# A fused attention and feed-forward kernel: crossbar transposes from the second batch on, and a new order of the first batch

## The chip, the cores and the metric

The kernel runs on one core of a Trainium2 chip. The metric is the time of one execution on the device, in microseconds (us). Lower is better. Most executions of one kernel agree within a few tenths of a per cent. A comparison always has runs of both kernels on the same chip in the same rounds.

The engines have short names in the profile: PE is the tensor engine, DVE the vector engine, ACT the scalar engine, POOL the engine that issues the loads here, SP the engine that issues stores and crossbar transposes. "Line" numbers such as L468 are lines of the kernel file in question, so they differ between kernels.

## The reference

```
# q, k, v: (8 batches, 12 heads, 448 rows, 64)
scores = q @ k^T / 8
attn   = max(scores, 0)**2 / 448
x      = (attn @ v), heads side by side        # 3584 rows x 768
out    = (max(x @ w_gate, 0) * (x @ w_val)) @ w_out      # 768 -> 1536 -> 768
```

Inputs and output are float32; the kernel computes in bfloat16 with float32 accumulation.

## The kernel before

The kernel has no fixed schedule. It makes a list of operations with their dependences, buffers and estimated durations; a small planner inside the kernel places them in time on paper, and the kernel then emits them in the planned order. Each engine executes its own instructions in exactly that order (in `e1b_head_only` below, DVE stands 4.33 us at one copy with its other work queued behind it), so a wrong estimate in the plan becomes a wait on the chip. This is the planner's part; `xfer` is what it believes that a transfer takes:

```python
def commit(self, op, s, e):
    op.start, op.eng = s, e
    d = op.engs[e]
    self.t[e] = s + d
    op.end = s + d
    if op.xfer:
        if e == "POOL":
            self.dmaq = max(self.dmaq, op.end + 1.3) + op.xfer
            op.end = self.dmaq + 0.7
            # (cut)
        else:
            op.end += 2.0 + op.xfer
```

q and k have to be transposed before the scores. For batches 0 to 2 PE does it (`transpose_quad`, four heads at a time, with a copy out of PSUM on DVE or ACT for each pair of heads). From batch `XBAR_FROM = 3` on the DMA crossbar does it: seven DVE copies bring a batch into pair order in one buffer (`pair`, there is only one), and two crossbar transposes, issued by SP, read it:

```python
def transpose_batch(b):
    # (cut)
    for s, t in enumerate(slot_order(b)):
        op = Op({"DVE": 0.36}, lambda s=s, t=t: emit_pair(s, t), deps=deps + perm[:1], delay=6.0,
                alloc=[pair] if s == 0 else [], reads=[st.buf])      # st.buf: the loaded q and k
        perm.append(op)
        others.append(op)
    # (cut)
    for i in range(2):
        op = Op({"SP": 0.3}, lambda i=i: emit_x(i), deps=perm + xo[:1], alloc=[st.tbuf] if i == 0 else [],
                reads=[pair], xfer=13.0)                              # the plan believes 2 + 13 us
        xo.append(op)
        others.append(op)
    for hp in range(HP):
        t_op[(b, hp)] = xo[1]                                         # scores wait for the second
```

There are two input buffers for q and k (`r_in = Res(2)`). The load of batch b+2 may start when batch b has been transposed, or, with the crossbar, when its seven copies are done.

After attention come the FFN products: groups of six matrix products (`g_ps`, `v_ps`) and groups of twelve (`o_ps`). They are PE's reserve of work for the times when attention has to wait; the FFN of a batch needs all value products of that batch.

## Time and profile before

| | before |
|---|---|
| time, median of 3 | 443.87 us (443.56 to 444.12) |
| span of the profiled execution | 442.0 us |
| PE busy | 428.8 us (97%) |
| batch 1's first transposes start | 37.99 us |
| PE's waits after that | one, 0.51 us |

The page's table of engines, and the row of the 40 slices for PE (each digit is the busy share of a slice of 11 us in tenths):

```profile
PE 428.8 (97%) x3092; PEld 228.9 (52%) x3092; DVE 222.2 (50%) x392; ACT 210.2 (48%) x354; POOL 44.2 (10%) x65
...
PE   6799999999999999999999999999999999999996
```

PE is the limit everywhere but in the first slices and the last. A change gains by giving PE less to do, or by a shorter head. PE's timeline (start, length, instructions; in brackets the idle time before and what ended it) shows the head, two groups of transposes, and the only later wait:

```profile
5.17 0.96 PE L332 MATMUL t_ps<-ident,qk 128*64 128x128 bf16 x14 [0.31 <-issue]
7.25 0.96 PE L332 MATMUL t_ps<-ident,qk 128*64 128x128 bf16 x14 [1.12 <-DMA qk<-in_q_dram]
...
9.20 0.98 PE L456 MATMUL s_ps<-qkT 64*128 64x192 bf16 x10 [0.72 <-ACT qkT L340]
11.98 1.70 PE L332 MATMUL t_ps<-ident,qk 128*64 128x128 bf16 x28 [1.80 <-DMA qk<-in_q_dram]
...
37.99 0.95 PE L332 MATMUL t_ps<-ident,qk 128*64 128x128 bf16 x28
...
62.17 0.95 PE L332 MATMUL t_ps<-ident,qk 128*64 128x128 bf16 x28
63.05 0.67 PE L554 MATMUL g_ps<-xT,wg_99 128*128 128x192 bf16 x6
```

```profile
142.95 0.37 PE L456 MATMUL s_ps<-qkT 64*128 64x448 bf16 x2 [0.51 <-ACT xT L525]
```

A length includes the time in which one group's end overlaps the next, so the cost of a group is read from start to start: the 28 transposes at 62.17 us cost 63.05 - 62.17 = 0.88 us. The same 28 at 11.98 us cost nearly twice as much, 1.64 us to the next start: PE ran at half rate there. (The view of stretches gives the granted clock as 1.00 from 12 to 14 us; the durations of the same instructions are the surer sign here.)

SP's timeline around the first crossbar transposes (batch 3's; the length is the time SP needs to hand them to the DMA engines, not the time to landing):

```profile
102.97 18.29 SPq L376 DMA_TRANSPOSE qkT<-pair  x2
...
183.18 4.33 SPq L376 DMA_TRANSPOSE qkT<-pair  x1
```

The view of the tile that these transposes read gives their landing: issued at 103.0 us amid loads, 15.6 us later; the second, at 107.8 us, 25.3 us later; the one at 183.2 us, with few loads around it, 6.6 us later.

### The profile page before, as it was taken

The numbers are of one execution on the slowest core, as the hardware profiler recorded it, in microseconds if no ns is written. First come the engines' busy times: TensorE is split into PE (matmuls) and PEld (weight loads), VectorE is DVE, ScalarE is ACT, GpSimd is POOL, SyncE is SP. The second block draws the span as 40 slices with busy tenths as digits, with TensorE's granted clock in tenths as the row PEclk, the third lists the DMA queues.
The fourth block names the chain that finished last, engine by engine and source line by source line (L and its number), as shares of the span: only waits on it lengthen the run. The fifth ranks groups of instructions, "written<-read, shape, count | busy, mean of one in ns | idle before, by whom it ended". The sixth has DMA issues, their size and how long they took to land.

```text
span 442.0 us, 7571 instructions
## 1 busy us (share of the span) xinstructions
PE 428.8 (97%) x3092; PEld 228.9 (52%) x3092; DVE 222.2 (50%) x392; ACT 210.2 (48%) x354; POOL 44.2 (10%) x65
## 2 busy tenths in 40 slices
PE   6799999999999999999999999999999999999996
PEld 2577775545454444544455444554445544555553
DVE  1676865656707654645753646635553456302210
ACT  3675656654536544544554555444553444332221
POOL 8336220004001100020001000010000000000000
PEclk9999999999999999999999999999999999999999
DMA  7999999707996990499044901390002200040014
GB/s 101 191 198 198 202 203 203 160 14 73 175 170 176 166 156 0 83 194 154 1 63 116 161 1 29 75 182 21 1 1 73 71 1 0 1 104 5 1 37 107
DMA packets 69699, 42.76 MB, mean 97 GB/s; under 512 B 29088, under 2 KB 66208, under 8 KB 69664
## 3 DMA queue, kind: packets, MB, share of 16 engines
q0 software_dynamic: 37824, 24.38, 39.2%
q1 hardware_dynamic: 31760, 17.80, 21.5%
q8 instruction: 24, 0.39, 0.4%
q10 hardware_dynamic: 80, 0.10, 0.1%
q14 instruction: 11, 0.09, 0.1%
HBM read 48.76 MB, written 11.01 MB: 135 GB/s over the span
## 4 chain that ended last, share of the span: by engine, by line
PE 95%; DMA 2%; DVE 1%; POOL 1%; ACT 1%; issue 0%; POOLq 0%; DVEq 0%
PE g_ps L554 26%; PE o_ps L606 25%; PE v_ps L554 25%; PE s_ps L513 7%; PE s_ps L456 7%; PE t_ps L332 2%; PE s_ps L462 2%; DMA qk<-in_q_dram 2%; PE s_ps L507 1%; POOL qk L239 1%; ACT xT L525 0%; DVE at L490 0%; DVE qkT L342 0%; DVE r_sb L474 0%; DVE o_sb L621 0%
## 5 line engine op out<-in xcount | busy, mean ns | idle before, releaser
L472 ACT ACTIVATE r_sb<-s_ps 128x896 bf16<-128x896 f32 (+5 forms) x161 | 107.3, 726 | 34.0 <-PE s_ps L456 19.7
L568 DVE TENSOR_TENSOR hT<-v_ps,g_sb 128x448 bf16<-128x448 f32 (+2 forms) x108 | 61.6, 570 | 113.4 <-PE v_ps L554 109.3
L490 DVE TENSOR_TENSOR at<-r_sb 128x896 bf16<-128x896 bf16 (+4 forms) x171 | 98.2, 609 | 24.2 <-ACT r_sb L472 24.0
L561 ACT ACTIVATE g_sb<-g_ps 128x448 bf16<-128x448 f32 (+2 forms) x104 | 53.1, 510 | 99.2 <-PE g_ps L554 97.0
L606 PEld LDWEIGHTS <-hT 128*128 128x128 bf16 x672 | 63.9, 98 | 48.5 <-issue 7.7
L474 DVE TENSOR_SCALAR r_sb<-s_ps 128x896 bf16<-128x896 f32 (+4 forms) x58 | 52.8, 933 | 38.0 <-PE s_ps L456 38.0
L619 ACT ACTIVATE o_sb<-o_ps 128x384 f32<-128x384 f32 (+1 forms) x55 | 26.8, 488 | 69.9 <-PE o_ps L606 68.9
L606 PE MATMUL o_ps<-wo_106,hT 128*128 128x384 bf16 x336 | 59.3, 326 | 0.0
L606 PE MATMUL o_ps<-wo_107,hT 128*128 128x384 bf16 x336 | 59.2, 326 | 0.0
L456 PE MATMUL s_ps<-qkT 64*128 64x448 bf16 (+2 forms) x324 | 38.1, 343 | 1.8 <-ACT qkT L340 0.7
L513 PE MATMUL s_ps<-at,vv 128*64 128x448 bf16 (+2 forms) x324 | 33.4, 345 | 0.0
L239 POOL DMA_DIRECT2D vv<-in_v_dram x20 | 14.2, 719 | 185.3 <-PE s_ps L513 140.7
L525 ACT CAST xT<-s_ps 128x896 bf16<-128x896 f32 (+2 forms) x26 | 21.7, 835 | 17.0 <-PE s_ps L513 17.0
L456 PEld LDWEIGHTS <-qkT 64*128 64x128 bf16 x324 | 12.4, 97 | 22.0 <-issue 15.9
L513 PEld LDWEIGHTS <-vv 128*64 128x64 bf16 x324 | 16.3, 113 | 14.5 <-issue 7.5
L554 PE MATMUL g_ps<-xT,wg_94 128*128 128x448 bf16 (+2 forms) x108 | 21.2, 333 | 0.0
L554 PE MATMUL g_ps<-xT,wg_96 128*128 128x448 bf16 (+2 forms) x108 | 21.2, 332 | 0.0
L554 PE MATMUL g_ps<-xT,wg_99 128*128 128x448 bf16 (+2 forms) x108 | 21.2, 332 | 0.0
L554 PE MATMUL g_ps<-xT,wg_97 128*128 128x448 bf16 (+2 forms) x108 | 21.2, 332 | 0.0
L554 PE MATMUL g_ps<-xT,wg_95 128*128 128x448 bf16 (+2 forms) x108 | 21.2, 332 | 0.0
L554 PE MATMUL g_ps<-xT,wg_98 128*128 128x448 bf16 (+2 forms) x108 | 21.2, 332 | 0.0
L554 PE MATMUL v_ps<-xT,wv_101 128*128 128x448 bf16 (+2 forms) x108 | 21.2, 332 | 0.0
(55 smaller groups left out, 336.8 us busy)
## 6 DMA issues: line engine op xcount, KB each, us to landing
out_dram<-o_sb SPq DMA_DIRECT2D x54, 192.0 KB, 2.7
vv<-in_v_dram POOLq DMA_DIRECT2D x14, 384.0 KB, 10.1
qk<-in_k_dram POOLq DMA_DIRECT2D x6, 672.0 KB, 15.8
qk<-in_q_dram POOLq DMA_DIRECT2D x6, 672.0 KB, 19.2
wo_106<-in_moe_w_out_dram POOLq DMA_DIRECT2D x1, 1152.0 KB, 16.0
wo_107<-in_moe_w_out_dram POOLq DMA_DIRECT2D x1, 1152.0 KB, 19.5
qk<-in_k_dram POOLq DMA_DIRECT2D x5, 224.0 KB, 10.4
qk<-in_q_dram POOLq DMA_DIRECT2D x5, 224.0 KB, 9.5
```

The lines of the kernel that those rows point to most:

```text
L239: op = Op({"POOL": 0.5 + 0.0004 * n_desc}, lambda: nc.gpsimd.dma_start(out=dst(), in_=src), deps=deps, alloc=alloc, xfer=kb / rate)
L456: nc.tensor.matmul(half_of(h2)[:, m * n:(m + 1) * n], lhsT=kq(1, j, h2, key_off(b) + c * 128, 128), rhs=kq(0, j, h2, self.c0, n), start=Tr ...
L472: nc.scalar.activation(dst, src, AF.Relu)
L474: nc.vector.tensor_scalar_max(dst, src, 0.0)
L490: lambda: nc.vector.tensor_tensor(self.at_tile(i), loc["r"][:, :2 * ne], loc["r"][:, :2 * ne], ALU.mult),
L513: nc.tensor.matmul(x_ps[o, j, :n], lhsT=st.vv[:, 4 * g + 2 * j + h2, 1 + c, :], rhs=self.at(j, c, h2), start=False, stop=(c == NC - 1))
L525: nc.scalar.copy(dst, loc["x"][:, :, :n])
L554: nc.tensor.matmul(ps, lhsT=w[c][:, kd, o:o + 128], rhs=st.xT[:, kd, cols], start=(kd == 0), stop=(kd == KD - 1))
L561: nc.scalar.activation(loc["gs"], loc["g_ps"], AF.Relu)
L568: nc.vector.tensor_tensor(hs["hT"][:, mf, t0:t0 + n], loc["v_ps"], loc["gs"], ALU.mult)
L606: nc.tensor.matmul(loc["o"], lhsT=hs["hT"][:, kf, ti * 128:(ti + 1) * 128], rhs=w_out_sb[hf][:, kf, :], start=(kf == 0), stop=(kf == KF - 1))
L619: nc.scalar.activation(out=dst, in_=src, func=AF.Copy, scale=float(out_scale))
```

## The change

The change wants to take batch 2's transposes off PE (`XBAR_FROM = 2`), and to shorten the head: transposes by pair of heads, so that a copy can start half a group earlier; a third buffer for the squared scores of the first part (`spare`); value products of the first batch in single PSUM banks; zero products between the first groups (`W2`) so that PE's clock stays up; and an order found by search. It also changes figures that the planner believes: 0.26 us instead of 0.2 between engines, shorter evictions, 9 us instead of 13 for a crossbar transpose, and 6 us for batch 2's. Batch 1's last value products are moved ahead of batch 2's scores (and batch 2's ahead of batch 3's), so that batch 1's FFN is free to run while the crossbar works.

```diff
-XBAR_FROM = 3
+XBAR_FROM = 2
...
-    LAT = 0.2
+    LAT = 0.26
...
-    def transpose_quad(b, g):
+    def transpose_pair(b, g, j):
...
         for s, t in enumerate(slot_order(b)):
-            op = Op({"DVE": 0.36}, lambda s=s, t=t: emit_pair(s, t), deps=deps + perm[:1], delay=6.0,
+            op = Op({"DVE": 0.36}, lambda s=s, t=t: emit_pair(s, t), deps=deps + perm[:1], delay=6.0 if b > 2 else 1.5,
...
             op = Op({"SP": 0.3}, lambda i=i: emit_x(i), deps=perm + xo[:1], alloc=[st.tbuf] if i == 0 else [],
-                    reads=[pair], xfer=13.0)
+                    reads=[pair], xfer=9.0 if b > 2 else 6.0)
...
-        return {"ACT": 0.18 + n / 1200.0, "DVE": 0.17 + n / 960.0}
+        return {"ACT": 0.10 + n / 1200.0, "DVE": 0.09 + n / 960.0}
...
-    load_heads(0, 0, H, "v")
+    load_heads(0, 4, 8, "v")
...
+    ORDER = ("T0 W2 T1 A0:0f A0:1 W2 A0:3 W2 A0:2 T2 T3 A1:0 A1:1f A1:3 T4 T5 A1:2 A2:0 A2:1f A2:2 VA0f A2:3 "
+             "B0:0 VA1f B0:3 VA2f B0:1f B0:2 / B1:0 B2:0 VB0f / / B2:1f / B1:2 B2:3 B1:3 B1:1 / / B2:2 VB1f VB2")
...
+            if b in (XBAR_FROM, XBAR_FROM + 1) and g == 0:
+
+                nb += 1
+                att.append((prev.pv(), nb))
+                xburst[prev.b] = nb
+                prev = None
```

More of the change, by code (lines that the diff above doesn't have):

```diff
@@ L39, in __init__ @@
         self.bias = bias
+        self.lat = 1.3
         self.start = self.end = None
 class Planner:
-    LAT = 0.2
+    LAT = 0.26
     NOUT = 8
     def __init__(self):
-        self.t = {"POOL": 1.0}
+        self.t = {"POOL": 1.35}
         self.ops = []
@@ L85, in commit @@
             if e == "POOL":
-                self.dmaq = max(self.dmaq, op.end + 1.3) + op.xfer
+                self.dmaq = max(self.dmaq, op.end + op.lat) + op.xfer
                 op.end = self.dmaq + 0.7
@@ L223, in bank, with spare @@
         return psum.tile([128, 512 if dt == FP32 else 1024], dt, name=name, tag="f", bufs=4)
+    AT = (2 * NC + 1) * 2 * S
+    def spare():
+        return pairs.tile([128, AT], BF16, name="spare")
     ident = const.tile([128, 128], BF16)
@@ L236, in identity, with dma_in @@
                                 fill=0.0, base=0, channel_multiplier=1)
-    def dma_in(dst, src, n_desc, kb, deps=(), alloc=(), rate=350.0):
-        op = Op({"POOL": 0.5 + 0.0004 * n_desc}, lambda: nc.gpsimd.dma_start(out=dst(), in_=src),
+    def dma_in(dst, src, n_desc, kb, deps=(), alloc=(), rate=380.0):
+        op = Op({"POOL": 0.58 + 0.0004 * n_desc}, lambda: nc.gpsimd.dma_start(out=dst(), in_=src),
                 deps=deps, alloc=alloc, xfer=kb / rate)
+        op.lat = 0.75 if n_desc <= 128 else 1.3
         pool_ops.append(op)
@@ L274, in load_heads @@
             bat[b] = Batch()
-            bat[b].buf = Buf(r_in, NT if b >= XBAR_FROM else NQ)
+            bat[b].buf = Buf(r_in, NT if b >= XBAR_FROM else HP)
             bat[b].vbuf = Buf(r_v, NQ * len(PARTS(b)))
@@ L287, in load_heads @@
         rows = lambda x: x[b, hs].rearrange("h (p t) d -> p h t d", t=NT)
-        rate = 290.0 if b == 0 else 340.0
+        rate = (240.0 if h0 == 4 else 290.0) if b == 0 else 340.0
         if "k" in what:
@@ L295, in load_heads @@
             v0 = dma_in(lambda: tile_of("vv", NC + 2)[0:64, hs, 1:NC + 2], rows(v)[:, :, 0:NC + 1], 64 * n, 64 * n,
-                        alloc=[st.vbuf] if h0 == 0 else [], rate=rate)
-            v1 = dma_in(lambda: tile_of("vv", NC + 2)[64:128, hs, 0:NC + 1], rows(v)[:, :, NC:NT], 64 * n, 64 * n, rate=rate)
+                        alloc=[st.vbuf] if h0 == 0 else [], rate=340.0)
+            v1 = dma_in(lambda: tile_of("vv", NC + 2)[64:128, hs, 0:NC + 1], rows(v)[:, :, NC:NT], 64 * n, 64 * n, rate=340.0)
             for h in range(h0, h0 + n):
@@ L319, with idle, emit_copy @@
     t_op = {}
-    def transpose_quad(b, g):
+    zeros = const.tile([128, 512], BF16)
+    def idle(n):
+        for _ in range(n):
+            nc.tensor.matmul(bank("w_ps"), lhsT=zeros[:, :128], rhs=zeros, start=True, stop=True)
+    def transpose_pair(b, g, j):
         st = bat[b]
-        ps = [Buf(r_f, 1), Buf(r_f, 1)]
+        ps = Buf(r_f, 1)
         box = {}
         def emit():
-            for j in range(2):
-                t_ps = bank("t_ps", BF16)
-                for i, t in enumerate(slot_order(b)):
-                    for h2 in range(2):
-                        nc.tensor.transpose(t_ps[64 * h2:64 * h2 + 64, i * 128:(i + 1) * 128],
-                                            st.qk[:, 4 * g + 2 * j + h2, t, :], ident)
-                box[j] = t_ps
-        def emit_copy(cp, j):
+            t_ps = box["t"] = bank("t_ps", BF16)
+            for i, t in enumerate(slot_order(b)):
+                for h2 in range(2):
+                    nc.tensor.transpose(t_ps[64 * h2:64 * h2 + 64, i * 128:(i + 1) * 128],
+                                        st.qk[:, 4 * g + 2 * j + h2, t, :], ident)
+        def emit_copy():
             dst = columns_of(b)[:, :, 2 * g + j, :].rearrange("p a (t c) -> p t a c", c=P2)
-            src = box[j][:, :2 * S].rearrange("p (t a c) -> p t a c", t=NT, a=2)
+            src = box["t"][:, :2 * S].rearrange("p (t a c) -> p t a c", t=NT, a=2)
             if cp.eng == "ACT":
@@ L342, in emit_copy @@
                 nc.vector.tensor_copy(dst, src)
-        deps = [d for h in range(4 * g, 4 * g + 4) for d in st.qk_op[h]] + [id_op]
-        op = Op({"PE": 1.0}, emit, deps=deps, alloc=ps, reads=[st.buf])
-        for j in range(2):
-            first = g == 0 and j == 0
-            cp = Op({"DVE": 0.65, "ACT": 0.92}, None, deps=[op],
-                    alloc=[st.tbuf] if first else [], reads=[ps[j]], prio=0, bias=-0.3)
-            cp.emit = lambda cp=cp, j=j: emit_copy(cp, j)
-            others.append(cp)
-            t_op[(b, 2 * g + j)] = cp
+        h = 4 * g + 2 * j
+        op = Op({"PE": 0.5 if g or b else 0.95}, emit, deps=list(st.qk_op[h]) + list(st.qk_op[h + 1]) + [id_op],
+                alloc=[ps], reads=[st.buf])
+        cp = Op({"DVE": 0.57, "ACT": 0.84}, emit_copy, deps=[op], alloc=[st.tbuf] if g == 0 and j == 0 else [],
+                reads=[ps], prio=0, bias=0.0)
+        others.append(cp)
+        t_op[(b, 2 * g + j)] = cp
         return op
@@ L364, in emit_pair @@
             if s == 0:
-                box["p"] = pairs.tile([128, HP, NT, 2, D], BF16, name="pair")
+                box["p"] = spare()[:, :HP * NT * 2 * D].rearrange("p (a t c d) -> p a t c d", a=HP, t=NT, c=2)
             nc.vector.tensor_copy(box["p"][:, :, s], st.qk[:, :, t, :].rearrange("p (a c) d -> p a c d", c=2))
@@ L390, in on_psum, with __init__ @@
     def on_psum(n):
-        return {"ACT": 0.18 + n / 1200.0, "DVE": 0.17 + n / 960.0}
+        return {"ACT": 0.10 + n / 1200.0, "DVE": 0.09 + n / 960.0}
     xop = {}
     class Part:
-        def __init__(self, b, g, c0, n, shared=None):
+        def __init__(self, b, g, c0, n, shared=None, home=None):
             self.b, self.g, self.c0, self.n = b, g, c0, n
@@ L405, in __init__ @@
             self.own = shared is None
-            self.box, self.at_buf, self.base = shared or ({}, Buf(r_at, 1), 0)
+            self.home = home
+            self.box, self.at_buf, self.base = shared or ({}, Buf(r_pair if home else r_at, 1), 0)
         def size(self):
@@ L444, in emit @@
                 if "at" not in box:
-                    box["at"] = apool.tile([128, (2 * NC + 1) * 2 * S], BF16, name="at")
+                    box["at"] = self.home() if self.home else apool.tile([128, AT], BF16, name="at")
                 if single:
@@ L488, in s @@
                 rel.append(o)
-            sq = Op({"DVE": 0.16 + 2 * ne / 1920.0},
+            sq = Op({"DVE": 0.08 + 2 * ne / 1920.0},
                     lambda: nc.vector.tensor_tensor(self.at_tile(i), loc["r"][:, :2 * ne], loc["r"][:, :2 * ne], ALU.mult),
@@ L494, in s, with pv @@
             return op
-        def pv(self):
+        def pv(self, split=False):
             b, g, n = self.b, self.g, self.n
             st = bat[b]
-            ps = Buf(r_s, 1)
+            ps = [Buf(r_f, 1), Buf(r_f, 1)] if split else [Buf(r_s, 1)]
             loc = {}
             def emit():
-                x_ps = bank_pair()
+                if split:
+                    loc["x"] = [bank("x1_ps"), bank("x1_ps")]
+                    x_of = lambda o, j: loc["x"][j][o, :n]
+                else:
+                    loc["x"] = bank_pair()
+                    x_of = lambda o, j: loc["x"][o, j, :n]
                 for j, h2, half in ((0, 0, 0), (0, 1, 1), (1, 0, 1), (1, 1, 0)):
@@ L506, in emit @@
                     o = slice(64 * h2, 64 * h2 + 64)
-                    nc.tensor.matmul(x_ps[o, j, :n], lhsT=st.vv[p, 4 * g + 2 * j + h2, (NC + 1) * (1 - half), :],
+                    nc.tensor.matmul(x_of(o, j), lhsT=st.vv[p, 4 * g + 2 * j + h2, (NC + 1) * (1 - half), :],
                                      rhs=self.at_tail(h2)[p], start=True, stop=False)
@@ L512, in emit @@
                             o = slice(64 * h2, 64 * h2 + 64)
-                            nc.tensor.matmul(x_ps[o, j, :n], lhsT=st.vv[:, 4 * g + 2 * j + h2, 1 + c, :],
+                            nc.tensor.matmul(x_of(o, j), lhsT=st.vv[:, 4 * g + 2 * j + h2, 1 + c, :],
                                              rhs=self.at(j, c, h2), start=False, stop=(c == NC - 1))
-                loc["x"] = x_ps
             dv = [d for h in range(4 * g, 4 * g + 4) for d in st.v_op[h]]
-            op = Op({"PE": 0.2 + 7 * n / 2400.0}, emit, deps=self.sq + dv, alloc=[ps], reads=[self.at_buf, st.vbuf])
@@ L520, in emit_copy @@
-            def emit_copy(cp):
+            op = Op({"PE": 0.2 + 7 * n / 2400.0}, emit, deps=self.sq + dv, alloc=ps, reads=[self.at_buf, st.vbuf])
+            def emit_copy(cp, j):
                 if not hasattr(st, "xT"):
                     st.xT = xpool.tile([128, KD, S], BF16, name="xT")
-                dst = st.xT[:, 2 * g:2 * g + 2, self.c0:self.c0 + n]
+                if split:
+                    dst = st.xT[:, 2 * g + j, self.c0:self.c0 + n]
+                    src = loc["x"][j][:, :n]
+                else:
+                    dst = st.xT[:, 2 * g:2 * g + 2, self.c0:self.c0 + n]
+                    src = loc["x"][:, :, :n]
@@ L524, in emit_copy @@
                 if cp.eng == "ACT":
-                    nc.scalar.copy(dst, loc["x"][:, :, :n])
+                    nc.scalar.copy(dst, src)
                 else:
-                    nc.vector.tensor_copy(dst, loc["x"][:, :, :n])
-            first = not hasattr(st, "x_buf")
-            if first:
-                st.x_buf = Buf(r_x, 2 * KF * len(PARTS(b)))
-            cp = Op(on_psum(2 * n), None, deps=[op], alloc=[st.x_buf] if first else [], reads=[ps])
-            cp.emit = lambda: emit_copy(cp)
@@ L534, in pv @@
-            others.append(cp)
-            xop.setdefault((b, self.c0), []).append(cp)
+                    nc.vector.tensor_copy(dst, src)
+            for j in range(len(ps)):
+                first = not hasattr(st, "x_buf")
+                if first:
+                    st.x_buf = Buf(r_x, 2 * KF * len(PARTS(b)))
+                cp = Op(on_psum(n if split else 2 * n), None, deps=[op], alloc=[st.x_buf] if first else [], reads=[ps[j]],
+                        prio=0 if split else 1)
+                cp.emit = lambda cp=cp, j=j: emit_copy(cp, j)
+                others.append(cp)
+                xop.setdefault((b, self.c0), []).append(cp)
@@ L575, in gv_ops @@
         vop = Op(pe, lambda: product("v_ps", w_val_sb), deps=xop[(b, c0)] + [wv_op[c]], alloc=[va], reads=[st.x_buf])
-        vmul = Op({"DVE": 0.17 + n / 960.0}, emit_mul, deps=[vop, grel], alloc=[hs["buf"]] if first else [],
+        vmul = Op({"DVE": 0.09 + n / 960.0}, emit_mul, deps=[vop, grel], alloc=[hs["buf"]] if first else [],
                   reads=[va, gs], prio=0)
@@ L665 @@
     load_heads(0, 0, 2, "k")
+    load_heads(0, 2, 2, "k")
     id_op = Op({"POOL": 0.35}, identity)
     pool_ops.append(id_op)
-    load_heads(0, 2, 2, "k")
     load_heads(0, 4, 4, "k")
+    load_heads(0, 0, 4, "v")
     load_heads(0, 8, 4, "k")
-    load_heads(0, 0, H, "v")
+    load_heads(0, 4, 8, "v")
     load_gv(0)
@@ L682 @@
     load_out(1)
-    load_heads(2, 0, H)
-    for b in range(3, B):
+    for b in range(2, B):
         load_heads(b, 0, H, "k")
@@ L687 @@
             load_heads(b - 1, 0, H, "v")
+        if b == 2:
+            load_heads(b, 0, H, "v")
         if b >= XBAR_FROM:
@@ L699, in T @@
         if b < min(B, XBAR_FROM):
-            att.append((transpose_quad(b, g), nb))
+            for j in range(2):
+                att.append((transpose_pair(b, g, j), nb))
     (ca, na), (cb, nbc) = PARTS(0)
-    A = [Part(0, 0, ca, na)]
-    A.append(Part(0, 1, ca, na, A[0].share()))
-    A.append(Part(0, 2, ca, na))
-    Bp = [Part(0, 0, cb, nbc, A[2].share()), Part(0, 1, cb, nbc), Part(0, 2, cb, nbc)]
-    def scores(pt, nxt=None, between=()):
-        for i in range(NC + 1):
-            att.append((pt.s(i, split=i == 1), nb))
-            if i == 2 and nxt is not None:
-                T(0, nxt)
-            if i == 1:
-                for x in between:
-                    att.append((x.pv(), nb))
@@ L720, in warm_up @@
-    def warm_up():
-        z = const.tile([128, 512], BF16, name="zeros")
-        nc.vector.memset(z, 0.0)
-        for _ in range(8):
-            nc.tensor.matmul(bank("w_ps"), lhsT=z[:, :128], rhs=z, start=True, stop=True)
-    att.append((Op({"PE": 3.0}, warm_up), nb))
-    T(0, 0)
-    for g in range(NQ):
-        scores(A[g], g + 1 if g + 1 < NQ else None)
-        nb += 1
-    att.append((A[0].pv(), nb))
-    nb += 1
-    scores(Bp[0], between=A[1:])
-    nb += 1
-    scores(Bp[1])
-    nb += 1
@@ L737, with W, first_zeros @@
-    att.append((Bp[0].pv(), nb))
-    scores(Bp[2])
-    nb += 1
-    att.append((Bp[1].pv(), nb))
+    A = [Part(0, g, ca, na, home=spare if g == 2 else None) for g in range(NQ)]
+    Bp = [Part(0, g, cb, nbc, A[g].share()) for g in range(NQ)]
+    def W(n, us):
+        if n:
+            att.append((Op({"PE": us}, lambda: idle(n), alloc=[Buf(r_f, 1)]), nb))
+            att[-1][0].reads = att[-1][0].alloc
+    def first_zeros():
+        nc.vector.memset(zeros, 0.0)
+        idle(8)
+    att.append((Op({"PE": 3.0}, first_zeros), nb))
@@ new lines @@
+    ORDER = ("T0 W2 T1 A0:0f A0:1 W2 A0:3 W2 A0:2 T2 T3 A1:0 A1:1f A1:3 T4 T5 A1:2 A2:0 A2:1f A2:2 VA0f A2:3 "
+             "B0:0 VA1f B0:3 VA2f B0:1f B0:2 / B1:0 B2:0 VB0f / / B2:1f / B1:2 B2:3 B1:3 B1:1 / / B2:2 VB1f VB2")
+    for x in ORDER.split():
+        part = {"A": A, "B": Bp}
+        single = x[-1] == "f"
+        if x == "/":
+            nb += 1
+        elif x[0] == "T":
+            att.append((transpose_pair(0, int(x[1]) // 2, int(x[1]) % 2), nb))
+        elif x[0] == "W":
+            W(int(x[1]), 0.25 * int(x[1]))
+        elif x[0] == "V":
+            att.append((part[x[1]][int(x[2])].pv(single), nb))
+        else:
+            att.append((part[x[0]][int(x[1])].s(int(x[3]), single), nb))
@@ L741 @@
     prev = Bp[2]
-    nb += 1
-    att.append((prev.pv(), nb))
     xburst[0] = calm = nb
@@ L750 @@
             pt = Part(b, g, 0, S)
+            if b in (XBAR_FROM, XBAR_FROM + 1) and g == 0:
+                nb += 1
+                att.append((prev.pv(), nb))
+                xburst[prev.b] = nb
+                prev = None
             for k0 in (0, NC):
```

## The prediction

> **What bounds the kernel now.** The tensor engine: the page's engine table gives PE 428.8 of 442.0 us (97%), VectorE and ScalarE about half. The stretches view shows PE without a gap from 38 us to the last product, but for one wait of 0.5 us at 142 us; the last 4.4 us only store. So the change can gain by work that PE no longer does after 38 us, and in the head before it.
>
> **The head.** In PE's timeline real work starts at 5.2 us and the first transposes of batch 1 at 38.0 us. At the warm start-to-start times of the later trace (0.031 us a transpose, 0.08 us a 192-column product, 0.50 us a group of six) this work would take 20 to 21 us: some 12 us are lost, to idle PE and to instructions at half rate (28 transposes took 1.70 us at 12 us, 0.88 us at 62 us). The Trainium skill ("TensorE: Matmul & The Clock Gate", Part 1) says that PE runs at half rate until it has been busy for about 3.4 us; the trace agrees with the half rate.
>
> **What the change does.**
> 1. Batch 2 moves from PE's transposes to the crossbar. Its three groups of 28 took 0.88 us each in step: -2.6 us on the critical path. VectorE gains seven copies of 0.35 us for some 0.62 us evictions: free.
> 2. Head: transposes by pair start the first copies earlier; a third buffer of squares; value products in single banks; six zero products keep PE clocked up. The first two copies were at 6.2 us (VectorE) and 8.2 to 9.1 us (ScalarE): I expect the first full scores 0.7 to 1 us earlier. The third transpose still waits for q of heads 4 to 7, which landed at 11.9 us. After that buffers, order and clock were the limit: the first part's value products ended at 24.4 us; I expect about 21.5. Then weights bind: by the DMA view the third chunk's value weights land at 30.6 us, and in the new order 3.9 us of PE work lie between their first use and batch 1's transposes. Those start at 34.5 us at the earliest; expected 35 instead of 38: -3 us.
> 3. The 0.5 us wait may go.
>
> **What it may cost.** Batch 2's crossbar transposes start after its VectorE copies, about 76 us, when batch 3's q and k still load, and those copies free the buffer for batch 4's loads. In the trace before, two transposes issued at 103.0 and 107.8 us amid loads landed 15.6 and 25.3 us later; a quiet one took 6.6 us. In the new order batch 2's first scores come about 59 us of PE work after batch 1's first transposes, about 94 us. With landing between 90 and 102 us, a stall of 0 to 8 us is possible; I count 1 us, as the order was tuned.
>
> **Sum.** 443.9 - 2.6 - 3 - 0.3 + 1 = about 438.8 us, 1.2% faster. Range 435.2 to 442.2 us. Faster by over 2% (below 435): 8%; within 2%: 90%; slower: 2%.
>
> **What would show it.** PE's transposes: 168 instead of 252, six more zero products; batch 1's first transpose near 35 us; shorter waits in the head; PE's waits naming batch 2's crossbar transposes near 94 us: none or short; the tail unchanged.
>
> **What would make it wrong.** A long stall on batch 2's or 3's crossbar transposes (no gain at all); weights landing later; PE at half rate in the head in spite of the zero products; or weights landing earlier, so that the head shrinks by over 5 us.

## The result

| | before | after |
|---|---|---|
| time, median of 4 | 443.72 us | 451.12 us (450.23 to 451.56) |
| ratio after / before | | 1.0167 (1.0144 to 1.0190) |
| span of the profiled execution | 442.0 us | 449.1 us |
| batch 1's first transposes start | 37.99 us | 34.90 us |
| longest wait of PE after that | 0.51 us | 9.94 us |
| last product group starts | 435.48 us | 442.72 us |

A ratio is the mean time of one kernel's fast runs over the mean of the other's fast runs of the same rounds, so it is not quite the ratio of the medians.

The kernel is slower, and the page shows one place: the ninth and tenth slices (90 to 112 us).

```profile
PE 428.7 (95%) x3014; PEld 224.7 (50%) x3014; DVE 232.2 (52%) x412; ACT 198.1 (44%) x339; POOL 45.3 (10%) x67
...
PE   6799999937999999999999999999999999999996
```

PE's timeline after, first the lines that answer to those of before, then the place of the loss:

```profile
7.36 0.96 PE L346 MATMUL t_ps<-ident,qk 128*64 128x128 bf16 x14 [1.37 <-DMA qk<-in_q_dram]
...
9.04 0.66 PE L468 MATMUL s_ps<-qkT 64*128 64x192 bf16 x6 [0.45 <-DVE qkT L355]
...
22.00 0.69 PE L530 MATMUL x_ps<-spare,vv 128*64 128x192 bf16 x12
...
34.90 0.95 PE L346 MATMUL t_ps<-ident,qk 128*64 128x128 bf16 x28
```

```profile
92.98 1.30 PE L577 MATMUL g_ps<-xT,wg_96 128*128 128x448 bf16 x6
104.22 1.30 PE L468 MATMUL s_ps<-qkT 64*128 64x448 bf16 x6 [9.94 <-DMA qkT<-spare]
105.46 2.42 PE L577 MATMUL v_ps<-xT,wv_102 128*128 128x448 bf16 x6
107.67 2.33 PE L577 MATMUL g_ps<-xT,wg_97 128*128 128x448 bf16 x6
109.84 1.30 PE L577 MATMUL v_ps<-xT,wv_103 128*128 128x448 bf16 x6
111.07 0.74 PE L468 MATMUL s_ps<-qkT 64*128 64x448 bf16 x6
111.75 1.31 PE L577 MATMUL g_ps<-xT,wg_97 128*128 128x448 bf16 x6
112.89 1.30 PE L577 MATMUL v_ps<-xT,wv_103 128*128 128x448 bf16 x6
```

PE stands still until 104.22 us for batch 2's transposed q and k. What follows is slow: from start to start the six scores cost 1.24 us, the next two groups 2.21 and 2.17 us; the same at 111.07, 111.75 us and after cost 0.68, 1.14 and 1.14 us. The view of stretches gives the granted clock as 0.50 from 100 to 105 us and 0.52 from 105 to 110 us. What SP and POOL did meanwhile:

```profile
75.84 11.20 SPq L387 DMA_TRANSPOSE qkT<-spare  x1
87.08 1.41 SPq L673 DMA_DIRECT2D out_dram<-o_sb  x2
88.53 42.91 SPq L387 DMA_TRANSPOSE qkT<-spare  x3
...
144.13 4.13 SPq L387 DMA_TRANSPOSE qkT<-spare  x1
```

```profile
63.33 0.75 POOL L246 DMA_DIRECT2D qk<-in_q_dram  x1
75.14 0.75 POOL L246 DMA_DIRECT2D qk<-in_k_dram  x1 [11.06 <-DVE spare L377]
...
81.69 1.49 POOL L246 DMA_DIRECT2D vv<-in_v_dram  x2 [5.07 <-PE s_ps L530]
```

The two transposes of batch 2 were issued at 75.84 and 88.53 us and landed, by the view of the tile, 20.9 and 15.6 us later: at 96.7 and just before 104.2 us. SP needed 11.2 us to hand over the first, against 4.1 us for the one at 144.13 us. At 75.14 us, straight after the seven copies had freed the input buffer, POOL issued batch 4's loads of q and k (they landed 15.7 and 19.5 us later), and at 81.69 us batch 3's v. Batch 3's q and k, issued at 62.59 and 63.33 us, were still on their way too (18.3 and 22.2 us, until 85.5 us). The landing of the second transpose, from the view of the tile between 88 and 89 us:

```profile
DMA to landing us min/median/max: 15.6/15.6/15.6
```

So the two spans differ by 7.1 us, and the trace accounts for 6.7 us of it:

| term | us |
|---|---|
| head: 34.90 - 37.99 | -3.1 |
| three groups of 28 transposes gone from PE, 0.88 each | -2.6 |
| the wait at 142 us gone | -0.5 |
| wait for batch 2's crossbar transposes | +9.9 |
| half rate after it: (1.24 - 0.67) + (2.21 - 1.14) + (2.17 - 1.14) | +2.7 |
| batch 1's first FFN group waits for its input at 81 us: 1.44 instead of 1.14 | +0.3 |
| sum | +6.7 |

### The profile page after: what moved, and what is told of

It is laid out like the page before. It is cut to its first block, busy times and chain, and to the rows that moved or that the text cites. A ratio compares the mean times of both kernels' runs of the same rounds, so it can differ in the third digit from the quotient of the medians.

```text
span 449.1 us, 7413 instructions
## 1 busy us (share of the span) xinstructions
PE 428.7 (95%) x3014; PEld 224.7 (50%) x3014; DVE 232.2 (52%) x412; ACT 198.1 (44%) x339; POOL 45.3 (10%) x67
## 4 chain that ended last, share of the span: by engine, by line
PE 92%; DMA 4%; DVE 1%; ACT 1%; issue 1%; SPq 0%; POOL 0%; ACTq 0%; POOLq 0%
PE o_ps L629 25%; PE v_ps L577 24%; PE g_ps L577 24%; PE s_ps L468 7%; PE s_ps L530 6%; DMA qkT<-spare 3%; PE s_ps L474 2%; PE t_ps L346 1%; PE s_ps L524 1%; DMA qk<-in_q_dram 1%; PE x_ps L530 1%; DVE qkT L355 0%; ACT r_sb L484 0%; PE w_ps L334 0%; POOL qk L246 0%
## 5 line engine op out<-in xcount | busy, mean ns | idle before, releaser
L484 ACT ACTIVATE r_sb<-s_ps 128x896 bf16<-128x896 f32 (+4 forms) x145 | 99.5, 740 | 46.6 <-PE s_ps L468 35.5
L502 DVE TENSOR_TENSOR at<-r_sb 128x896 bf16<-128x896 bf16 (+4 forms) x163 | 93.4, 611 | 21.3 <-ACT r_sb L484 20.9
L486 DVE TENSOR_SCALAR r_sb<-s_ps 128x896 bf16<-128x896 f32 (+5 forms) x73 | 63.2, 894 | 46.7 <-PE s_ps L468 46.3
L246 POOL DMA_DIRECT2D vv<-in_v_dram x22 | 15.4, 708 | 187.0 <-PE s_ps L530 177.3
L530 PE MATMUL s_ps<-at,vv 128*64 128x448 bf16 x252 | 27.8, 357 | 0.0
L546 ACT CAST xT<-s_ps 128x896 bf16<-128x896 f32 (+1 forms) x22 | 19.6, 891 | 12.8 <-PE s_ps L530 12.8
L530 PEld LDWEIGHTS <-vv 128*64 128x64 bf16 x324 | 15.6, 109 | 14.0 <-issue 7.0
L577 PE MATMUL v_ps<-xT,wv_102 128*128 128x448 bf16 (+2 forms) x108 | 22.3, 344 | 0.0
L577 PE MATMUL g_ps<-xT,wg_97 128*128 128x448 bf16 (+2 forms) x108 | 22.2, 344 | 0.0
## 6 DMA issues: line engine op xcount, KB each, us to landing
wo_106<-in_moe_w_out_dram POOLq DMA_DIRECT2D x1, 1152.0 KB, 15.7
```

The costliest lines, as they stand in the source:

```text
L246: op = Op({"POOL": 0.58 + 0.0004 * n_desc}, lambda: nc.gpsimd.dma_start(out=dst(), in_=src), deps=deps, alloc=alloc, xfer=kb / rate)
L484: nc.scalar.activation(dst, src, AF.Relu)
L486: nc.vector.tensor_scalar_max(dst, src, 0.0)
L502: lambda: nc.vector.tensor_tensor(self.at_tile(i), loc["r"][:, :2 * ne], loc["r"][:, :2 * ne], ALU.mult),
L530: nc.tensor.matmul(x_of(o, j), lhsT=st.vv[:, 4 * g + 2 * j + h2, 1 + c, :], rhs=self.at(j, c, h2), start=False, stop=(c == NC - 1))
L546: nc.scalar.copy(dst, src)
```

## The experiments

Each run below has its edit against the changed kernel unless said otherwise; all gave correct results.

### Is it the crossbar in batch 2, or the whole new plan?

`e1_head_only`: crossbar from batch 3 on, as before, and everything else as changed.

```diff
-XBAR_FROM = 2
+XBAR_FROM = 3
```

> The changed kernel with the crossbar from batch 3 on, as before; all else as changed (undo one part). Theory A (the loss is the wait for batch 2's crossbar transposes and the half-rate clock after it; the new head is good for 3 us): no wait of PE over 1.5 us after 35 us, batch 1's first transposes at 35 us, time 440 to 441.5 us, about 10 us under the changed kernel. Rival B (the new order of the whole plan, with its new latencies, loses time elsewhere): time stays above 444 us.

Measured: two fast runs of 446.63 and 445.92 us, ratio 1.0087 (1.0045 to 1.0129), where theory A had 440 to 441.5 us and rival B over 444 us. So theory A in this form fell, and something in the new plan, other than batch 2's transposes, lost time. The other two runs were slow: one of 452.76 us, and the profiled one of 916.49 us, whose products took about twice their time throughout. That profile cannot be used, and why this one execution was so slow stays open. The kernel was therefore run again as `e1b_head_only`:

> The same kernel as the first run of this study (crossbar from batch 3 on, all else as changed), again, because the profile of that run fell into an execution at under half the usual rate, and its fast executions were 0.9% slower than the kernel before where theory A expected 0.7% faster. Theory A3 (the same fault one batch later: the change also tells the plan 9 us for batch 3's transposes, where the kernel before told it 13 us, so their reader is placed too early): one wait of PE of 5 to 9 us, naming the crossbar's result, between 115 and 140 us, followed by half-rate products; head as in the changed kernel (batch 1's first transposes at 35 us). Rival B (losses spread over the plan): no single wait over 3 us.

Measured: 448.0 us median, ratio 1.0116 (1.0078 to 1.0154). The head was good (batch 1's first transposes at 35.53 us), but no wait of PE names the crossbar. There are two waits of 3.0 and 2.3 us, and both name DVE. DVE's timeline explains the first:

```profile
153.94 1.08 DVE L486 TENSOR_SCALAR r_sb<-s_ps 128x896 bf16<-128x896 f32 x1
159.35 0.36 DVE L377 COPY spare<-qk 128x768 bf16<-128x768 bf16 x1 [4.33 <-DMA qkT<-spare]
159.62 1.69 DVE L502 TENSOR_TENSOR at<-r_sb 128x896 bf16<-128x896 bf16 x3
```

```profile
158.54 0.36 PE L468 MATMUL s_ps<-qkT 64*128 64x448 bf16 x1
161.90 0.82 PE L468 MATMUL s_ps<-qkT 64*128 64x448 bf16 x5 [3.00 <-DVE hT L591]
162.66 2.42 PE L577 MATMUL g_ps<-xT,wg 128*128 128x448 bf16 x6
164.87 1.76 PE L577 MATMUL v_ps<-xT,wv 128*128 128x448 bf16 x6
166.47 1.30 PE L577 MATMUL g_ps<-xT,wg 128*128 128x448 bf16 x6
```

A copy of the next batch into the pair buffer stood in DVE's program before the crossbar had finished reading that buffer. DVE waited 4.33 us for it, in order, so it did not free the PSUM banks behind it, and PE ran out of banks: 3.0 us idle, then half rate (2.21 us for the group at 162.66 us and 1.60 us for the next, instead of 1.14). The same happened at 209.6 us: DVE waited 3.94 us, PE 2.3 us, and the two groups from there on took 1.64 and 2.24 us instead of 1.14. Together this is 3.0 + 1.5 + 2.3 + 1.6 = 8.4 us. Theory A3 named the right cause, the plan's figure of 9 us, and the wrong carrier, so its expectation missed. The transposes of batch 3 and 4 landed 14.2 to 24.5 us after issue in this run. `e8_head_told` tests the cause by giving the old figure back:

```diff
-XBAR_FROM = 2
+XBAR_FROM = 3
...
-                    reads=[pair], xfer=9.0 if b > 2 else 6.0)
+                    reads=[pair], xfer=13.0)
```

> Crossbar from batch 3 on, and the plan told 13 us for each transpose, as in the kernel before; the rest as changed: the head alone, with the old figure. Theory A3: the single wait goes, time 440 to 441.5 us where the kernel before takes 443.7 (ratio 0.992 to 0.995). Rival B: no better than the kernel before.

Measured: 441.51 us median (440.99 to 444.34), ratio 0.9984 (0.9951 to 1.0018). The waits on DVE are gone: PE is without a gap from 130 to 160 us, and the whole rest has two waits of 0.4 us. The span of the profile is 439.7 us, 8.6 us under `e1b_head_only`; batch 1's first transposes start at 34.72 us, 3.3 us earlier than in the profile of the kernel before. In the times the gain over the kernel before is within the noise: the expected ratio of 0.992 to 0.995 was not reached. The median is 1.3 us under that of the kernel before in the same rounds, and one of the four runs took 444.34 us. The trace shows the shorter head; that all of it reaches the whole time is not shown. The 6.5 us between the medians of this run and `e1b_head_only` (1.3% in the ratios, whose intervals are far apart) are outside the noise, and the edit between them changes nothing but the figure.

### Would the plan have hidden the transposes, had it known how long they take?

`e3_told`: the crossbar from batch 2 on, and the plan told 12 us instead of 6 us for batch 2's two transposes.

```diff
-                    reads=[pair], xfer=9.0 if b > 2 else 6.0)
+                    reads=[pair], xfer=9.0 if b > 2 else 12.0)
```

> The changed kernel, but the plan is told 12 us for each of batch 2's two crossbar transposes instead of 6 us; nothing else is edited. PE's program then puts ten more groups of FFN products ahead of batch 2's first scores. Theory A1 (the transposes take some 28 us in this place whatever PE does, and the plan placed their reader too early): transposes land at 102 to 106 us as before, PE's wait for them falls from 9.9 us to under 1.5 us, the half-rate stretch goes, time 438 to 440 us. Rival A2 (there is not enough other work, or the work just moves and PE runs dry later): the wait comes back in another place, and time stays above 445 us.

Measured: 439.22 us median, ratio 0.9932 (0.9901 to 0.9963). The transposes were as slow as in the changed kernel (issued at 75.56 and 88.33 us, landed 21.0 and 15.4 us later, the second at 103.7 us). But batch 2's first scores now stand at 105.28 us in PE's timeline, behind ten more groups of FFN products, and PE does not wait for them:

```profile
104.05 1.30 PE L577 MATMUL g_ps<-xT,wg 128*128 128x448 bf16 x6
105.28 0.74 PE L468 MATMUL s_ps<-qkT 64*128 64x448 bf16 x6
```

This confirms A1: the work to hide the transposes was there, and the plan did not use it because it believed 6 us. A wait of 1.6 us at 210 us is left, of the same kind as in `e1b_head_only`; no half-rate products follow it (the next group takes 1.13 us).

### Why were they slow: loads, or the queue?

`e4_hold`: before batch 4's loads of q and k, POOL copies one element out of batch 2's transposed q and k into the tile that the load is going to overwrite. The load cannot be issued until the second transpose has landed. PE's program is unchanged, instruction for instruction.

```diff
+        if b == 4 and "k" in what:
+            def hold():
+                nc.gpsimd.tensor_copy(tile_of("qk", NT)[64:65, 0, 0, 0:1], bat[2].qkT[64:65, 1, 0, 0:1])
+            pool_ops.append(Op({"POOL": 0.3}, hold, deps=[bat[2].xo[1]], alloc=[st.buf]))
... (cut: the load of batch 4's k no longer takes the buffer itself)
```

> The changed kernel, but batch 4's loads of q and k (and so batch 3's v, which is next in the same queue) may only be issued when batch 2's second crossbar transpose has landed: one element is copied from its result into the tile that the load overwrites. PE's program is unchanged. Theory C1 (the transposes are slow because the loads that were let loose at 75 us share the DMA engines with them): the first lands at most 14 us after its issue instead of 20.9, both by 95 to 97 us instead of 104.2, PE's wait falls to under 3 us, time 439 to 442 us. Rival C2 (the transposes are slow by themselves or because of the stores between them and the loads of batch 3 that were already under way): landing stays over 101 us, wait over 7 us, time over 448 us.

Measured: 437.58 us median, ratio 0.9886 (0.9855 to 0.9918). POOL, SP and PE of this run:

```profile
94.25 0.36 POOL L300 COPY qk<-qkT 1x1 bf16<-1x1 bf16 x1 [29.87 <-DVE hT L598]
94.91 0.75 POOL L246 DMA_DIRECT2D qk<-in_k_dram  x1 [0.30 <-POOL qk L300]
```

```profile
76.13 8.98 SPq L393 DMA_TRANSPOSE qkT<-spare  x1
...
86.43 38.81 SPq L393 DMA_TRANSPOSE qkT<-spare  x3
```

```profile
93.28 1.30 PE L584 MATMUL g_ps<-xT,wg 128*128 128x448 bf16 x6
94.51 0.74 PE L475 MATMUL s_ps<-qkT 64*128 64x448 bf16 x6
95.18 1.31 PE L584 MATMUL v_ps<-xT,wv 128*128 128x448 bf16 x6
```

And the landing of the second transpose, from the view of the tile between 86 and 87 us:

```profile
DMA to landing us min/median/max: 7.7/7.7/7.7
```

The transposes landed 13.7 and 7.7 us after issue: at 89.8 and 94.1 us, seven and ten us earlier than in the changed kernel, and the time is below the 439 to 442 us expected. (The profile puts POOL's copy down to DVE; it starts some 0.2 us after the landing, which is what it was made to wait for.) The first still had batch 3's loads beside it. PE does not wait for them at all, and no half-rate products follow. This confirms C1 and refutes C2: with the same instructions on PE, DVE and SP, holding back the loads alone (batch 4's q and k, and batch 3's v behind them) brought the second transpose's time to landing from 15.6 to 7.7 us and the first's from 20.9 to 13.7 us. The Trainium skill ("DMA: Bandwidth & Descriptors", "Queues, rings and completion order") says that each DMA engine takes turns between the queues it has work for, a packet at a time. The landing times agree with such sharing (15.6 us beside loads, 7.7 us without), and so do the packets that the DMA view counts: from 89 to 95 us in the changed kernel, with the first transpose and loads both under way, the queue of the loads moved 1163 packets and SP's queue, which carries the transposes and the stores, 1167: one for one. From 87 to 94 us in `e4_hold`, with no load under way, SP's queue moved 3578. So it got about 195 packets a microsecond beside loads and 511 without them.

`e5_back_to_back` tests the other suspect, the two stores between the transposes in SP's queue:

```diff
-        for i in range(2):
+        if b == 2:
+            op = Op({"SP": 0.6}, lambda: (emit_x(0), emit_x(1)), deps=perm, alloc=[st.tbuf], reads=[pair, pair], xfer=14.3)
+            xo = [op, op]
+            others.append(op)
+        for i in range(2 if b > 2 else 0):
```

> The changed kernel with batch 2's two transposes issued one behind the other; in the changed kernel two stores of results stand between them in the queue (1.4 us of its time). Theory C1 (loads in flight are what makes them slow): the second is issued 1.4 us earlier and lands 0 to 2 us earlier, PE's wait is 8 to 10 us, time 449 to 451 us. Rival C3 (the order of the queue, stores ahead of the second transpose, makes most of the delay): wait under 5 us, time under 446 us.

Measured: 449.9 us median, ratio 1.0164 (1.0147 to 1.0181), the same as the changed kernel; PE waited 9.6 us, until 103.62 us. The two stores between the transposes made no difference that counts.

`e2_xbar_only` asks the reverse: the kernel before with the crossbar from batch 2 on, nothing else of the change.

```diff
-XBAR_FROM = 3
+XBAR_FROM = 2
...
     load_heads(2, 0, H)
+    transpose_batch(2)
```

> The kernel before with the crossbar from batch 2 on and nothing else of the change: old head, old figure of 13 us, and the last value products of batch 1 still behind batch 2's first scores. Theory A (the transposes take 20 to 30 us from about 76 us on, whoever plans them, and what hides that is FFN work of batch 1, which needs those value products first): PE has only two pairs of output products left and waits 15 to 22 us for the crossbar at about 83 us, then runs at half rate; time 455 to 465 us. Rival B (the wait belongs to the changed plan's figures alone): wait under 5 us, time under 446 us.

Measured, one run, whose state is unknown: 462.6 us beside 443 us.

```profile
77.73 4.55 PE L606 MATMUL o_ps<-wo,hT 128*128 128x384 bf16 x27
99.76 1.67 PE L456 MATMUL s_ps<-qkT 64*128 64x448 bf16 x8 [17.48 <-DMA qkT<-pair]
```

PE waited 17.5 us, with the plan told 13 us, so rival B is out. PE's program fits theory A: batch 1's last value products and its FFN stood behind batch 2's scores, and PE had nothing else to do from 82.3 us on. But the transposes themselves were not slow for 20 to 30 us here. SP issued them only at 84.1 and 92.9 us, after six stores whose hand-over ended at 83.9 us, and they landed 11.0 and 6.8 us later; so some 7 us of the way to the landing at 99.7 us was spent in SP's queue. That the move of those value products ahead, which is part of the change, is needed is argued from this order; no run tests it alone.

### Does the wait cost twice?

The account above gives 2.7 us to half-rate products after the wait. `e6_warm40` puts 40 zero products into the wait:

```diff
                 xburst[prev.b] = nb
                 prev = None
+                if b == 2:
+                    att.append((Op({"PE": 0.0}, lambda: idle(40), deps=[t_op[(2, 0)]]), nb))
```

> The changed kernel with 40 zero products put just ahead of batch 2's first scores in PE's program (8.5 us at full rate, less than the wait of 9.9 us); all else, the wait included, as it was. Theory D1 (the wait costs twice: 9.9 us idle and then about 2.7 us because PE runs at half rate until it has been busy again): the transposes still land near 104 us, the products after them take the full-rate times (448-column group of six 1.14 us instead of 2.2), time 448 to 449 us. Rival D2 (the slow products after the wait come from something else, such as operands or buffers): they stay slow, time 451 us or more.

Measured: 448.38 us median, ratio 1.0137 (1.0105 to 1.0168). The zero products ended at 101.8 us, PE then waited another 2.2 us, and the first two groups after it were again at half rate (1.23 and 2.13 us), the third no longer. So this was half a test, and `e9_warm50` repeats it with `idle(50)`:

> As the run with 40 zero products, which left 2.2 us of idle PE behind them and still 3.4 us of half-rate products; now 50 of them (10.65 us at 0.213 us each), so that they end about when the transposes land. Theory D1 (the clock falls because PE is idle): no half-rate product follows, batch 2's first six score products take 0.67 us in step instead of 1.24, and the whole is 2 to 3 us under the changed kernel (ratio to the kernel before 1.010 to 1.012). Rival D2 (the products behind the wait are slow for another reason): they stay slow and the ratio stays over 1.014.

```profile
94.13 10.96 PE L334 MATMUL w_ps<-zeros 128*128 128x512 bf16 x50
105.01 0.74 PE L468 MATMUL s_ps<-qkT 64*128 64x448 bf16 x6
105.69 1.31 PE L577 MATMUL v_ps<-xT,wv 128*128 128x448 bf16 x6
106.83 1.30 PE L577 MATMUL g_ps<-xT,wg 128*128 128x448 bf16 x6
```

Measured: 449.69 us median, ratio 1.0153 (1.0124 to 1.0181). The trace confirms D1 for the products: the scores take 0.68 us and the next groups 1.14 us, all at full rate. The time does not confirm the size: the ratio lies on the rival's side of the expectation (over 1.014), and the intervals of this ratio and of the changed kernel's overlap. Part of the reason is that the 50 products end at 105.0 us, 1.4 us after the second transpose had landed in this run (issued at 88.8 us, 14.8 us to landing), which eats half of the gain. That the wait brings half rate is shown; that it is worth 2.7 us rests on the trace's own durations.

### The zero products in the head, and the version that is left

`e4b_hold` is `e4_hold` again, with more rounds; `e10_hold_no_fill` is the same without the six zero products (the three `W2` taken out of `ORDER`); `e11_hold_told8` is the same with 8 us instead of 6 us told for batch 2's transposes.

> The version with batch 4's loads held until batch 2's transposes have landed, again, with more rounds: ratio to the kernel before 0.985 to 0.991, about 6 us under it, the size that the prediction gave to head, transposes and the small wait together.

> The held version without the six zero products between the first transposes and scores (the eight at the start stay). Theory F1 (they keep PE's clock up and are worth their time): batch 1's first transposes start 0.5 to 2 us later than in the held version, time 0.5 to 2 us more. Rival F2 (PE waits there for q of heads 4 to 7 anyway and the fillers change nothing): within 0.5 us of the held version.

> The held version, and the plan told 8 us for batch 2's transposes instead of 6, so that batch 2's first scores stand some 4 us later in PE's program: in the held version they landed only 0.4 us before they were read. If that small margin costs time in some executions, this is 0.5 to 1.5 us faster and its runs lie closer together; if not, equal within 0.5 us, or slower by a new wait elsewhere.

| run | median | range | ratio to before |
|---|---|---|---|
| e4b_hold | 438.10 us | 437.31 to 439.66 | 0.9896 (0.9875 to 0.9916) |
| e10_hold_no_fill | 438.31 us | 437.77 to 439.43 | 0.9904 (0.9884 to 0.9924) |
| e11_hold_told8 | 437.79 us | 437.12 to 438.19 | 0.9890 (0.9872 to 0.9908) |

The six zero products do nothing measurable: without them batch 1's first transposes start at 34.56 us, with them at 35.06 us. In both profiles some of the early transposes ran at half rate. F2 holds, F1 fell. The larger figure for batch 2's transposes gives no gain outside the noise, though its six runs lie closer together. All three beat both the kernel before and the changed one, by about 1% and 2.7% (0.989 / 1.0167 = 0.973, an estimate across rounds).

## Why the prediction was wrong

The prediction had 438.8 us and a range of 435.2 to 442.2 us; measured were 451.12 us. Point by point:

- **Crossbar instead of PE for batch 2, -2.6 us: right.** The trace has 168 transposes instead of 252, and the three groups cost 0.88 us each.
- **Head, -3 us, batch 1's first transposes at 35 us: right in size.** They start at 34.90 us, and at 33.8 to 35.5 us in the profiles of the other runs with this head. Details of the reasoning were off, so the agreement of the number is in part luck. The first full scores came at 9.04 us instead of 9.20, not 0.7 to 1 us earlier, because the second pair's transposes still waited for q (until 7.36 us). The first part's value products ended at 22.6 us (22.00 plus 0.62 to the next start), not 21.5 us. The weights did not bind: the third chunk's value weights landed at 29.8 us, PE first used them at 30.95 us without a wait, and it was PE's own work, without a gap from 20.5 us on, that led to 34.90 us. (In four other runs with this head PE waited 0.2 to 1.3 us for value weights, at 25 to 27 us.) And the zero products were credited with keeping the clock up; run `e10_hold_no_fill` shows no gain from them.
- **The wait at 142 us: gone, as expected.**
- **The failing step: "a stall of 0 to 8 us is possible; I count 1 us, as the order was tuned".** The mechanism was seen: the copies free the buffer for batch 4's loads, transposes amid loads had taken 15.6 and 25.3 us, and the scores would be wanted at about 94 us. They were wanted at 94.28 us (104.22 less the wait of 9.94). But the transposes landed at 104.2 us, outside the 90 to 102 us given, and the term in the sum was 1 us where 9.9 us were measured. The trace before allowed a better figure: the pair issued at 103.0 us was finished only 30 us later (107.8 + 25.3), which from 76 us gives 106 us. What was trusted instead was that "the order was tuned". `e3_told` shows that the order rested on a belief of 6 us.
- **A term left out: half rate after the wait**, 2.7 us by the trace. The prediction had quoted the clock rule for the head and did not apply it to the stall. The Trainium skill ("TensorE: Matmul & The Clock Gate", "What's actually happening") gives both directions of it: full rate only after sustained work, half rate after an idle window. The trace agrees: clock 0.50 after the wait, and products at half rate for 5.6 us (104.22 to 109.84 us).

With 9.9 + 2.7 us in place of 1 us the prediction's own sum is 443.9 - 2.6 - 3 - 0.3 + 12.6 = 450.6 us. And with the loads held, so that the wait is gone, the chip gave 437.6 and 438.1 us, 4.3 and 5.0 us under the medians of the kernel before in the same rounds, where the prediction's three gains add up to 5.9 us. So the gains were real, in sum about 1 us smaller than predicted; one term was mis-sized and one was missing.

What stays open: how much of the first transpose's 20.9 us is due to batch 3's loads, which were already under way, and how much to batch 4's (with batch 4's held it still took 13.7 us); and the one execution of 916 us.

## What to carry to other kernels

Where a plan decides the order of in-order engines, a transfer's duration in it is part of the program: take it from a trace in the place where it will run, beside the loads that run there, and not from a quiet one. When a change moves a buffer's release forward, ask what the release lets loose and what that collides with; a one-element copy that ties the load to the end of the critical transfer took about 12 us off here (ratios to before of 0.9886 and 1.0167). And count a long stall of the tensor engine twice: the idle time, and the half-rate products after it (here 2.2 us of idle time and more were followed by them, 1.6 us in `e3_told` was not).

## What the Trainium skill lacked or had wrong

- "TensorE: Matmul & The Clock Gate", "What's actually happening": half rate is said to follow an idle window of about 3.4 us. Here 2.2 us of idle PE (`e6_warm40`, 101.8 to 104.0 us) were followed by two groups at half rate, and so were 3.0 and 2.3 us (`e1b_head_only`, at 162 and 210 us); 1.6 us (`e3_told`, at 210 us) and 0.5 us (before, at 142 us) were not.
- "DMA: Bandwidth & Descriptors", "Rules for kernel authors": a transpose next to ordinary DMAs "needs nothing". That held for correctness in every run; what the loads cost in time is not said there. Here a crossbar transpose of half a batch landed 6.6 us after its issue when it was quiet, 7.7 us with the loads held back, and 15.6 to 25.3 us beside loads (kernels before and after), and SP needed 11 to 12 us for each of batch 2's two instead of 4 us to hand it over.
- No page was found that gives the second way in which a slow transpose stops PE: a DVE copy that waits for the crossbar's source buffer blocks DVE in order, and PE runs out of PSUM banks (`e1b_head_only`: 4.3 us of DVE, 3.0 us of PE).
